# A listed order for all tasks, rounds of 768 and 1024 tokens, and sign bits by halfwords

## The chip, the cores and the metric

The kernel runs on one core of a Trainium2 chip. The metric is the device time of one execution in microseconds (us), the median of several runs. Five engines work side by side, each in the order in which its instructions were written: TensorE (PE in the profile, with weight loads as PEld) for matrix products into PSUM, VectorE (DVE) and ScalarE (ACT) for elementwise work, GpSimd (POOL) and SyncE (SP), which here only issue DMAs. Engines wait for each other through semaphores.

## The reference

```python
def _attn_ref(q, k, v, cap):                      # q, k, v: (4, 12, 448, 64)
    scores = (1 / sqrt(64)) * q @ k.T
    scores = cap * np.tanh(scores / cap)
    scores = scores - max(scores)
    attn = exp(scores); attn = attn / (sum(attn) + 1e-09)
    return attn @ v

def _moe_ref(x, w1, w2, w3, w_out):               # x: (1792, 768)
    a = x @ w1                                    # (1792, 1024)
    b = x @ w2
    h = a * b @ w3                                # w3: (1024, 1024)
    return h @ w_out                              # (1792, 768)
```

The heads of the attention's result are laid side by side to give x (4 batches of 448 tokens, 768 columns). Since nothing nonlinear stands between w3 and w_out, the kernel multiplies these two first.

## The kernel before, in words

**Work.** The 48 heads are taken as 24 pairs. For a pair, TensorE makes scores in tasks `S` (each float32 number is split into a high and a low part in the fp32r format, three products of the four are kept), ScalarE takes tanh (`H`) and exp (`E`), TensorE multiplies with v (`V`, `VJ`) and sums the exponentials (`T`, `Y`), a reciprocal goes through DRAM (`R0` to `R3`), VectorE scales (`N0`), and `N` stores the pair's 128 x 448 block to `x_dr`. Beside this, `O`, `Z` and `W` pieces bring w_out, w3, w1 and w2 from float64 words: a piece is loaded (`load`), its two 32-bit words are turned into one float (`low`, `sign`, `top`, `join`), and split into high and low (`high`, `out`). Tasks `C` multiply w3 with w_out and `D`, `DS` store the result.

**Rounds.** The products with w1 and w2 use Strassen's scheme with seven products, over two halves of the 768 channels and two blocks of tokens. A round covers two blocks: round 0 the batches 0 and 1, round 1 the batches 2 and 3, so a block has 448 tokens and a matmul 448 columns. `plan_xprep` loads a round's x from `x_dr`, forms the sums and splits them; `plan_moe` runs, for each of 8 column blocks m, seven products of three tasks `P` with three matmuls each, and combines them (`eM1`, `eo11`, ...), and `U` stores a*b to `u_dr`. Round 0 runs beside the end of the attention, round 1 after it; the split weights are stored to `w_dr` (`WS`) in round 0 and loaded again (`w1g`) in round 1.

**Last product.** `plan_out` takes 7 tiles of 256 tokens: loads from `u_dr` (`q`), sums (`s`), splits (`ha`, `la`), seven products of 4 tasks `p`, sums and stores to the output (`w`). Tile 4 takes its tokens from the ends of all four batches.

**Order.** Nothing of this is in loops at run time. Each step is a task with an engine (some with a second engine to choose), a duration, a key and needs. `Plan.run` plays the tasks through a model of the engines and writes each one's instructions when its engine takes it, the smallest key first; `SHIFTS` moves keys of single tasks. So the order of each engine's instructions is set when the program is built. TensorE works with four tile shapes: 128 x 128 (`C`, `P`, `p`), 64 rows x 128 (`S` on 128 keys), 64 x 64 (`S` on the last 64 keys, `VJ`) and 128 x 32 (`V`, `T`, `Y`). Stores named in `SHARED` can go by the SP queue or the GpSimd queue.

Of the kernel before, what the change touches and what calls it, by code (L numbers as in the profile page):

```python
# [37 lines left out]
class Slots:  # L38
# [9 lines left out]
    def close(self):  # L48
        self.uses[self.closed :] = sorted(
            self.uses[self.closed :], key=lambda x: (x[0] + x[2].shift, x[1])  # L50
        )
        for i in range(max(self.closed, self.n), len(self.uses)):
            new = self.uses[i][2]
            new.needs.extend(x for x in self.uses[i - self.n][3] if x is not new)
        self.closed = len(self.uses)


class Plan:
# [34 lines left out]
    def run(self, goals):  # L93
# [3 lines left out]
        for i, t in enumerate(self.tasks):  # L97
            t.key = (t.key + t.shift, i)
# [47 lines left out]
def program(  # L146
# [38 lines left out]
    SH = S // 2  # L185
    NRAW, NRT, NXS, NEV, NF = 3, 6, 5, 5, 6
# [3 lines left out]
    SIGN = -0x80000000  # L190
# [3 lines left out]
    const = ctx.enter_context(tc.tile_pool(name="const", bufs=1))  # L194
# [7 lines left out]
    ncap_sb = const.tile([P, 1], F32, name="ncap_sb")  # L202
    acap_sb = const.tile([P, 1], F32, name="acap_sb")
    wide_sb = const.tile([P, 1], F32, name="wide_sb")
    tsc_sb = const.tile([P, 1], F32, name="tsc_sb")
    ones = const.tile([P, P], F32, name="ones")
    ones2 = const.tile([P, P], F32, name="ones2")

# [23 lines left out]
    def put(name, eng, ns, key, emit, needs=(), lat=0.0, alt=(), after=()):  # L232
# [6 lines left out]
        done[name].shift = shifts.get(name, 0.0)  # L239
# [4 lines left out]
    class Piece:  # L244
# [7 lines left out]
        def load(self, pool):  # L252
# [3 lines left out]
            self.lo16 = self.raw.bitcast(U16)[:, : self.n, 1]  # L256
# [45 lines left out]
    def plan_piece(nm, x, key, lead, first=(), whole=True):  # L302

        n = x.n / PC
        for st, eng, ns, fn, needs, lat, alt in (
# [5 lines left out]
            ("sign", "DVE", 75 + 400 * n, x.sign, ("low",), 0, ()),  # L311
# [64 lines left out]
    att = ExitStack()  # L376
    qkp = att.enter_context(tc.tile_pool(name="qkp", bufs=2))
# [231 lines left out]

    def plan_X(pr):  # L610
# [19 lines left out]
        def total():  # L630
# [4 lines left out]
            for x, part in enumerate(parts):  # L635
                for n in range(4):
# [3 lines left out]
                        lhsT=ones[:, :32],  # L640
# [7 lines left out]
        def tail():  # L648
            for n in range(4):
# [3 lines left out]
                    lhsT=ones2[:, quarter(pr, j).start :][:, :32],  # L653
# [92 lines left out]
        def store():  # L746
            queue[0].dma_start(x_dr[pr], r[1])
# [4 lines left out]
        t = put(f"N{pr}", "SP", 450, end + 5, store, [f"N0{pr}"], 4500)  # L752
        use["x", pr].append(t)

    def plan_general(pr):

        def emit():
# [60 lines left out]
            queue[0].dma_start(x_dr[pr], xf)  # L818
# [14 lines left out]
    RT0, RWIN = (145, 328.18), (167.44, 104.0)  # L833
# [124 lines left out]
    def plan_xprep(r):  # L958

        tiles = {}  # L960
# [8 lines left out]
        def load(nm, kt, src, key, needs):  # L969
            x = nm, kt  # L970

            def emit():
                tiles[x] = xsp.tile([P, 512], F32, tag="xs", name=f"xs{r}{nm}{kt}")[:, :S]
                queue[0].dma_start(tiles[x], src)
# [5 lines left out]
        def keep_sum(kt):  # L980
            tiles["t1", kt] = ext[0].tile([P, S], F32, tag=f"t{kt}", name=f"t{kt}")

        def split(name, nm, kt, key, needs):
            i = op(name)

            def dst(x):
# [3 lines left out]
                return xt[r, i][:, kt, x, :S]  # L990

            def new(t):
# [3 lines left out]
                f"X{r}_{i}_{kt}", lambda: tiles[nm, kt], dst, S, key,  # L996
# [4 lines left out]
        def total(name, kt, to, a, b, key, needs):  # L1001
            def into():
# [6 lines left out]
                ALU.subtract, S, key, needs, [use["xs", r, x, kt] for x in {to, a, b}],  # L1009
# [3 lines left out]
        for kt in range(HX):  # L1013
# [14 lines left out]
            def keep(kt=kt):  # L1028
                queue[0].dma_start(t_dr[r, kt], tiles["a0", kt])
# [3 lines left out]
        for kt in range(HX):  # L1033
# [8 lines left out]
            total("T2", kt, "t1", "b1", "t1", key, [f"X{r}b1{kt}", f"X{r}T1{kt}" if r and kt else f"X{r}t1{kt}"])  # L1042
# [7 lines left out]
    def plan_moe(r, m):  # L1050
        box, ev, nm = {}, {}, f"{r}_{m}"
# [12 lines left out]
        def copy(name, bank, key, needs):  # L1064
            def emit(cp):
                ev[name] = evp.tile([P, S], F32, tag="ev", name=f"{name}{nm}")
                cp(ev[name], box[bank][:, :S])  # L1067

            evac(
                name, "ACT", 430, key, lambda: emit(nc.scalar.copy), needs, [bank], [name], True,  # L1070
                [("DVE", 540, lambda: emit(nc.vector.tensor_copy))],
            )

        def both(name, key, to, a, b, op, needs, banks=()):
            def emit():
                x = box[a][:, :S] if a in box else ev[a]
                y = box[b][:, :S] if b in box else ev[b]
                nc.vector.tensor_tensor(ev[to], x, y, op=op)

            evac(name, "DVE", 535, key, emit, needs, banks, sorted({x for x in (to, a, b) if x not in "ab"}))  # L1080

        def store(name, b, key, needs):
            def emit():
                queue[0].dma_start(u_dr[m, :, b * S : (b + 1) * S], ev[name])
# [4 lines left out]
        for i, p in enumerate(XORD):  # L1089
            bank = "a" if p in (1, 6, 7, 4) else "b"  # L1090
            new = p in (1, 2, 5)
            for kt in range(HX):

                def emit(p=p, i=i, kt=kt, bank=bank, new=new):
                    if new and kt == 0:
                        box[bank] = ps_o.tile([P, 512], F32, tag=tag[bank], name=f"pab{nm}_{p}")
                    for z, (a, c) in enumerate(((0, 0), (1, 0), (0, 1))):
                        nc.tensor.matmul(  # L1098
                            box[bank][:, :S],
                            lhsT=w_op(r, m, i)[:, a, kt, :],  # L1100
                            rhs=xt[r, i][:, kt, c, :S],
# [13 lines left out]
                t = put(f"P{nm}_{i}_{kt}", "PE", 612, key, emit, need)  # L1115
# [105 lines left out]
    def plan_C(n):  # L1221

        for nh in range(2):
# [30 lines left out]
            def evac(cp, box=box, c=c, nh=nh):  # L1254
                c[0] = evp.tile([P, S], F32, tag="ev", name=f"c{n}_{nh}")[:, :NH]
# [70 lines left out]
    def plan_out(t):  # L1326
# [4 lines left out]
        if t == 4:  # L1331
            at = [[(h * S + 3 * P, S - 3 * P), ((2 + h) * S + 3 * P, S - 3 * P)] for h in range(2)]
        else:
            r, i = (0, t) if t < 3 else (1, (0, 0, 0, 0, 0, 1, 2)[t])
            at = [[((2 * r + h) * S + i * P, P)] for h in range(2)]

        def load_quadrant(a, b):
            nm = f"A{a + 1}{b + 1}"

            def load():  # L1340
                ru[nm] = xsp.tile([P, HF, P], F32, tag="xs", name=f"{nm}_{t}")
                x = 0
                for t0, n in at[a]:
                    queue[0].dma_start(
                        ru[nm][:, :, x : x + n],
                        u_dr[b * HF : (b + 1) * HF, :, t0 : t0 + n].rearrange("m p t -> p m t"),
                    )
                    x += n
# [420 lines left out]
```

## Time and profile before

| what | value |
|---|---|
| median of 3 runs | 565.93 us (565.09 to 569.05) |
| the profiled execution's own time | 567.21 us |
| its span in the profile | 565.4 us |
| granted TensorE clock, mean | 0.996 |
| instructions | 10168 |
| DMA | 131.08 MB, mean 232 GB/s |

The span runs from the first to the last instruction of the profiled execution; some 1.8 us of its time lie outside. Busy time counts an instruction from its start to its end, and matmuls overlap each other; the chain of waits instead follows the work that ended last, and its pieces run from one start to the next.

### The profile page before, as it was taken

Reading aid. Unit: us, or ns where it says so; the run is one execution under the profiler, and the core shown is the slowest. Engines: PE = TensorE matmul, PEld = TensorE weight load, DVE = VectorE, ACT = ScalarE, POOL = GpSimd, SP = SyncE. Lnnn points to the kernel's source line nnn. Section 1 sums busy time; section 2 is a strip of 40 time slices with the busy share of each in tenths; the row PEclk is TensorE's granted clock in tenths of the full one; section 3 lists DMA queues with packets and bytes.
Section 4 is the critical chain, followed back from the end, with each engine's and each line's share of the span. In section 5 each row is a group of like instructions: output and inputs, shape, how many; then the busy total and the mean of one; then the engine's idle time right before and its main releaser. Section 6 shows DMA issues by size and latency. Waiting matters only on the chain.

```text
span 565.4 us, 10168 instructions
## 1 busy us (share of the span) xinstructions
PE 548.5 (97%) x3660; PEld 426.7 (75%) x3660; DVE 433.0 (77%) x874; ACT 342.6 (61%) x545; POOL 82.1 (15%) x150
## 2 busy tenths in 40 slices
PE   6999999999999999999999899999999999999994
PEld 3354558977576556667578889899999999999994
DVE  5998999687989999998987898765522676875531
ACT  6998998487978999887854654422211353344120
POOL 0000011101131111212213120111011001111311
PEclk9999999999999999999999999999999999999998
DMA  8678777758897876977579877899886233553311
GB/s 277 172 254 277 240 233 252 244 182 261 283 329 261 272 255 236 353 254 290 197 271 348 321 253 245 274 340 300 295 291 261 89 108 102 179 148 107 85 70 64
DMA packets 62510, 131.08 MB, mean 232 GB/s; under 512 B 12738, under 2 KB 40770, under 8 KB 60914
## 3 DMA queue, kind: packets, MB, share of 16 engines
q1 hardware_dynamic: 51746, 78.65, 44.2%
q0 software_dynamic: 10704, 51.68, 24.3%
q8 instruction: 31, 0.51, 0.4%
q14 instruction: 29, 0.24, 0.1%
HBM read 88.46 MB, written 41.77 MB: 230 GB/s over the span
## 4 chain that ended last, share of the span: by engine, by line
PE 73%; issue 9%; DVE 7%; DMA 5%; ACT 3%; POOL 1%; SPq 0%; POOLq 0%; DVEq 0%; ACTq 0%
PE pab L1098 35%; PE m L1452 13%; PE pv L555 7%; PE s L501 6%; PE pc L1233 6%; DMA r<-r_dr 3%; PE sum L638 2%; DMA r_dr<-z 1%; PE s L488 1%; PE pv L571 1%; PE sum L651 1%; ACT p L514 1%; POOL out_dram L1497 1%; DVE wt L344 1%; ACT p L517 1%
## 5 line engine op out<-in xcount | busy, mean ns | idle before, releaser
L517 ACT ACTIVATE p<-p,ncap_sb,acap_sb 128x896 f32<-128x896 f32 x84 | 92.6, 1138 | 0.1
L514 ACT ACTIVATE p<-s,tsc_sb 128x896 f32<-128x896 f32 x84 | 82.3, 1008 | 8.8 <-PE s L501 5.9
L1233 PEld LDWEIGHTS pc<-wo,w3t 128*128 128x128 f32 x384 | 65.6, 188 | 12.1 <-issue 5.9
L1233 PE MATMUL pc<-wo,w3t 128*128 128x384 f32 x384 | 73.3, 342 | 0.4 <-DVE wo L300 0.4
L1098 PE MATMUL pab<-x0T,wt 128*128 128x448 f32 x288 | 64.8, 371 | 2.4 <-ACT M L1067 2.3
L501 PE MATMUL s<-hl 64*128 64x448 f32 x432 | 58.9, 396 | 5.7 <-ACT hl L447 4.4
L1098 PE MATMUL pab<-x1T,wt 128*128 128x448 f32 x288 | 63.5, 368 | 0.1
L501 PEld LDWEIGHTS s<-hl 64*128 64x128 f32 x432 | 38.0, 190 | 33.6 <-ACT p L514 9.9
L555 PE MATMUL pv<-p,v 128*32 128x448 f32 x576 | 62.6, 546 | 0.6 <-ACT p L517 0.4
L1098 PEld LDWEIGHTS pab<-x0T,wt 128*128 128x128 f32 x288 | 52.8, 188 | 13.5 <-ACT M L1067 3.4
L1452 PE MATMUL m<-bT,ot 128*128 128x384 f32 x336 | 61.9, 334 | 0.0
L1452 PEld LDWEIGHTS m<-bT,ot 128*128 128x128 f32 x336 | 58.6, 188 | 0.1
L1098 PEld LDWEIGHTS pab<-x1T,wt 128*128 128x128 f32 x288 | 53.9, 188 | 5.8 <-ACT U L1067 0.4
L1098 PE MATMUL pab<-x0B,wt 128*128 128x448 f32 x216 | 48.7, 370 | 0.0
L1098 PE MATMUL pab<-x1B,wt 128*128 128x448 f32 x216 | 48.2, 368 | 0.0
L1452 PE MATMUL m<-bB,ot 128*128 128x384 f32 x252 | 47.1, 334 | 0.0
L1098 PEld LDWEIGHTS pab<-x0B,wt 128*128 128x128 f32 x216 | 39.7, 188 | 7.2 <-issue 1.7
L1384 ACT CAST ot<-A 128x512 fp32r<-128x512 f32 x40 | 23.6, 621 | 35.1 <-DVE A L1363 27.7
L1452 PEld LDWEIGHTS m<-bB,ot 128*128 128x128 f32 x252 | 44.0, 188 | 0.0
L1098 PEld LDWEIGHTS pab<-x1B,wt 128*128 128x128 f32 x216 | 40.5, 188 | 4.1
L1067 ACT COPY M<-pab 128x448 f32<-128x448 f32 x27 | 14.3, 531 | 39.4 <-PE pab L1098 39.2
L555 PEld LDWEIGHTS pv<-p,v 128*32 128x32 f32 x576 | 15.5, 109 | 28.8 <-issue 18.6
(143 smaller groups left out, 801.7 us busy)
## 6 DMA issues: line engine op xcount, KB each, us to landing
raw_w<-in_moe_w_dram SPq DMA_DIRECT2D x48, 384.0 KB
w_dr<-wt POOLq DMA_DIRECT2D x42, 384.0 KB, 4.5
wt<-w_dr POOLq DMA_DIRECT2D x10, 1536.0 KB, 7.7
kq<-in_kq_dram SPq DMA_DIRECT2D x23, 450.0 KB
raw_wo<-in_moe_w_out_dram SPq DMA_DIRECT2D x16, 384.0 KB
A<-u_dr SPq DMA_DIRECT2D x24, 256.0 KB
v<-in_v_dram SPq DMA_DIRECT2D x24, 224.0 KB
r<-r_dr SPq DMA_DIRECT2D x48, 112.0 KB
```

The source lines that it names most:

```text
L344: nc.vector.tensor_tensor(dst(1), src(), dst(0), op=ALU.subtract)
L488: nc.tensor.matmul(box[0][quarter(pr + n, j), n, :S], lhsT=raw_t[pr + n][at, QO + S + KM :], rhs=raw_t[pr + n][at, QO : QO + S], start=Tru ...
L501: nc.tensor.matmul(box[0][:, j, :S], lhsT=hl[at, a, S + (i - 1) * P : S + i * P], rhs=hl[at, c, :S], start=(z == 0), stop=(z == 2),)
L514: nc.scalar.activation(p, box[0][:, :, :S], AF.Tanh, scale=tsc_sb)
L517: nc.scalar.activation(p_t[pr, i], p_t[pr, i], AF.Exp, scale=acap_sb, bias=ncap_sb)
L555: nc.tensor.matmul(pv_t[pr][n * 32 : (n + 1) * 32, :S], lhsT=v_t[pr][:, 3 * j + i - 1, g * 32 : (g + 1) * 32], rhs=p_t[pr, i][:, j, :], st ...
L638: nc.tensor.matmul(box[1][n * 32 : (n + 1) * 32, :SH], lhsT=ones[:, :32], rhs=part[:, j, g * SH : (g + 1) * SH], start=(x == 0), stop=(x = ...
L1067: cp(ev[name], box[bank][:, :S])
L1098: nc.tensor.matmul(box[bank][:, :S], lhsT=w_op(r, m, i)[:, a, kt, :], rhs=xt[r, i][:, kt, c, :S], start=(new and kt == 0 and z == 0), stop ...
L1233: nc.tensor.matmul(box[0][:, :NH], lhsT=w3t[n][:, a, jt, :], rhs=wo[jt][:, c, ns], start=(jt == 0 and z == 0), stop=(jt == KF - 1 and z == 2),
L1384: copy(ot[j][:, q % 3, 0], ru[src])
L1452: nc.tensor.matmul(box[banks[m]][:, :NH], lhsT=ot[q // 3][:, q % 3, a, k, :], rhs=bt[RHS[m]][:, k, c, :], start=(new and k == 0 and z == 0 ...
```

## The change

The planner no longer chooses: all tasks are listed by name in the order in which they are written, with the engine after a slash where it is not the first one. There is one list up to the end of the attention and a second one for what follows. The rounds get blocks of 384 and of 512 tokens: round 0 takes the first 384 tokens of the batches 0 and 1, round 1 the whole batches 2 and 3 and, at the end of each block, the last 64 tokens of batch 0 or 1. The sign bits of a piece are masked from the upper halfword of the high word into the upper halfword of the low word, by an instruction with one tensor operand. The core of the diff:

```diff
+    SW = (384, 512)
+    OVER = S - SW[0]
+    UO = (0, SW[0], 2 * SW[0], 2 * SW[0] + SW[1])
...
-    shifts = {} if general else {
-        x.split(":")[0]: float(x.split(":")[1]) for x in SHIFTS.split()
-    }
+    part = iter(SEQUENCE.split("|"))
+
+    def run(goals):
+
+        if general:
+            plan.run(goals)
+            return
+        for x in next(part).split():
+            name, _, eng = x.partition("/")
+            opts = done[name].opts
+            opts[eng or next(iter(opts))][1]()
...
-            self.lo16 = self.raw.bitcast(U16)[:, : self.n, 1]
+            half = self.raw.bitcast(U16)[:, : self.n]
+            self.lo16, self.hi16 = half[:, :, 1], half[:, :, 3]
...
         def sign(self):
-            nc.vector.scalar_tensor_tensor(
-                self.lo, self.hi, SIGN, self.lo, op0=ALU.bitwise_and, op1=ALU.bitwise_or
-            )
+            nc.vector.tensor_scalar(self.lo16, self.hi16, 0x8000, None, op0=ALU.bitwise_and)
...
+    def keep_values(pr, x):
+
+        if pr >= PH:
+            queue[0].dma_start(x_dr[pr, :, :S], x)
+            return
+        queue[0].dma_start(x_dr[pr, :, : SW[0]], x[:, : SW[0]])
+        queue[0].dma_start(x_dr[pr + PH, :, S:], x[:, SW[0] :])
...
         def store():
-            queue[0].dma_start(x_dr[pr], r[1])
+            keep_values(pr, r[1])
...
                         nc.tensor.matmul(
-                            box[bank][:, :S],
+                            box[bank][:, :W],
                             lhsT=w_op(r, m, i)[:, a, kt, :],
-                            rhs=xt[r, i][:, kt, c, :S],
+                            rhs=xt[r, i][:, kt, c, :W],
...
-        if t == 4:
-            at = [[(h * S + 3 * P, S - 3 * P), ((2 + h) * S + 3 * P, S - 3 * P)] for h in range(2)]
-        else:
-            r, i = (0, t) if t < 3 else (1, (0, 0, 0, 0, 0, 1, 2)[t])
-            at = [[((2 * r + h) * S + i * P, P)] for h in range(2)]
+        r, i = (0, t) if t < 3 else (1, t - 3)
+        at = [[((2 * r + h) * S + i * P, P)] for h in range(2)]
+        if t == 6:
+            at = [[((x + h) * S + SW[0], OVER) for x in (2, 0)] for h in range(2)]
...
+SEQUENCE = """
+ld0 O0_1load O0_0load ld1 ldv0 O1_0load ldv1 ld2 h0_0/DVE l0_0 h0_1 cap S0_1 l0_1 O0_1low H0_1 S0_2
+O0_1sign O0_1top H0_2 S0_3 O0_1join O0_0top O1_1load E0_1 O0_0low S0_0 O0_0sign O0_0join H0_3
...
+P0_0_1_1 W2A21top eM1_0_0 W1S4 P0_0_1_2 E16_1 X0_2_1l P0_0_2_0 eo11_0_0 X0t12 P0_0_2_1 H16_0
+W2A21low N12 P0_0_3_0 l18_0 P0_0_3_1 O15 R114 E16_0 P0_0_3_2 W2A21sign R214 R115 S17_1 ld19 E16_3
+W2A21join S17_2 R215 X0_5_2h/DVE X0_4_1l WS0_5 eM5_0_0 V16_1 X0_5_2l W3A11load H17_1 W1_2l V16_2
...
+e422 p5_7_1 ha48/DVE w4M5 s6A12A12A11 p5_1_3 w3o12 p5_6_1 e5M1 p5_4_0 ha45 p4_4_3 ha46 p5_6_2 e421
...
+"""
```

Smaller edits that come with it: `x_dr` and `t_dr` get rows of 512 tokens, the evacuations and the x preparation use the round's width `W`, each quadrant of the last product is one load, the tiles `ones` and `ones2` shrink and live in the attention's pool. The second program in the file, for a large `cap`, is not entered with these inputs.

## Rows read from the trace of the kernel before

**Rows 1.** The page's first part: busy time, share of the span, instructions.
```profile
PE 548.5 (97%) x3660; PEld 426.7 (75%) x3660; DVE 433.0 (77%) x874; ACT 342.6 (61%) x545; POOL 82.1 (15%) x150
```

**Rows 2.** Windows by stage: length, each engine's busy time, granted clock, DMA share, GB/s.
```profile
0.00:40.00 40.00, 34.76 (x305) 17.10 (x305) 31.57 (x80) 35.16 (x45) 0.87 (x5) 1.00 0.73 233
40.00:95.00 55.00, 54.56 (x491) 30.42 (x491) 51.20 (x118) 52.04 (x73) 4.10 (x8) 1.00 0.80 251
95.00:195.00 100.00, 98.93 (x777) 70.61 (x776) 87.17 (x182) 78.94 (x123) 17.37 (x32) 1.00 0.78 260
195.00:351.00 156.00, 153.60 (x1000) 112.18 (x999) 143.00 (x284) 112.96 (x184) 29.83 (x51) 1.00 0.78 279
351.00:451.00 100.00, 99.94 (x484) 90.44 (x483) 53.09 (x100) 27.94 (x56) 12.05 (x22) 1.00 0.75 263
```

**Rows 3.** Chain of waits, 205 to 262 us: start, duration in us, what, matmuls.
```profile
206.15 1.41 PE s L501 x12
207.55 0.81 PE pab L1098 x3
...
212.06 0.52 PE sum L638 x8
...
213.44 0.38 PE sum L651 x8
...
218.16 0.91 PE s L488 x8
219.07 0.80 PE s L501 x6
...
230.82 2.39 PE pv L555 x24
...
239.36 6.27 PE pab L1098 x30
```

**Rows 4.** Chain of waits over the whole span, three of its pieces.
```profile
17.50 1.27 PE sum L638 x24
...
47.54 0.72 PE pc L1233 x3
...
461.53 69.18 PE m L1452 x399
```

**Rows 5.** Chain of waits, 395 to 440 us, in round 1.
```profile
394.85 45.25 PE pab L1098 x219
```

**Rows 6.** Timeline of TensorE, 0 to 12 us: start, us, line, tile, idle before.
```profile
4.40 0.74 PE L501 MATMUL s<-hl 64*128 64x448 f32 x2 [4.40 <-ACT hl L447]
...
7.60 1.77 PE L488 MATMUL s<-kq 64*64 64x448 f32 x8
```

**Rows 7.** Timeline of TensorE, 290 to 295 us.
```profile
292.58 0.56 PE L651 MATMUL sum<-p,ones 128*32 128x224 f32 x8
293.07 0.86 PE L1098 MATMUL pab<-x0T,wt 128*128 128x448 f32 x3
```

**Rows 8.** Timeline of TensorE, 550 to 566 us, its last row.
```profile
556.01 1.73 PE L1452 MATMUL m<-bB,ot 128*128 128x384 f32 x9
```

**Rows 9.** Groups by line and shape: count, busy us, mean ns, idle before.
```profile
L286 DVE SCALAR_TENSOR_TENSOR raw_w<-raw_w 128x384 int32<-128x384 int32 x48 | 26.1, 550 | 0.7 <-ACT raw_w L280 0.6
...
L275 DVE TENSOR_SCALAR raw_w<-raw_w 128x384 int32<-128x384 int32 x16 | 5.6, 352 | 0.2
...
L447 ACT CAST hl<-kq 128x576 fp32r<-128x576 f32 x1 | 0.7, 671 | 1.7 <-DMA kq<-in_kq_dram 1.7
```

**Rows 10.** Line 905, the weight stores: durations in ns as least, median, most.
```profile
L905 POOL DMA_DIRECT2D w_dr<-wt x42: 539/539/1199, 146.4 to 330.8; - x42
L905 SPq DMA_DIRECT2D w_dr<-wt x7: 320/331/380, 231.0 to 308.9; - x7
L905 SPq EVENT_SEMAPHORE  x6: 17/17/17, 230.4 to 306.3; - x6
```

**Rows 11.** Waits, longest first: us in total, times, longest us.
```profile
POOL w_dr L905 <- DVE wt L344: 64.3, 29, 9.5
...
POOL x_dr L747 <- DVE xf L744: 63.8, 15, 9.0
```

More of the change, by code (lines that the diff above doesn't have):

```diff
@@ L97, in run @@
         for i, t in enumerate(self.tasks):
[L98 removed]
+            t.key = (t.key, i)
             t.left = 0
@@ L376, in program @@
     att = ExitStack()
+    const = att.enter_context(tc.tile_pool(name="const", bufs=1))
+    ncap_sb = const.tile([P, 1], F32, name="ncap_sb")
+    acap_sb = const.tile([P, 1], F32, name="acap_sb")
+    wide_sb = const.tile([P, 1], F32, name="wide_sb")
+    tsc_sb = const.tile([P, 1], F32, name="tsc_sb")
+    ones = const.tile([P, 32], F32, name="ones")
+    ones2 = const.tile([P, 2, 32], F32, name="ones2")
     qkp = att.enter_context(tc.tile_pool(name="qkp", bufs=2))
@@ L751, in plan_X @@
         use["x", pr].append(t)
-        t = put(f"N{pr}", "SP", 450, end + 5, store, [f"N0{pr}"], 4500)
+        t = put(f"N{pr}", "SP", 450 if pr >= PH else 900, end + 5, store, [f"N0{pr}"], 4500)
         use["x", pr].append(t)
@@ L958, in plan_xprep @@
     def plan_xprep(r):
-        tiles = {}
+        tiles, W = {}, SW[r]
         def op(name):
@@ L972, in emit @@
             def emit():
-                tiles[x] = xsp.tile([P, 512], F32, tag="xs", name=f"xs{r}{nm}{kt}")[:, :S]
-                queue[0].dma_start(tiles[x], src)
+                tiles[x] = xsp.tile([P, 512], F32, tag="xs", name=f"xs{r}{nm}{kt}")[:, :W]
+                queue[0].dma_start(tiles[x], src[:, :W])
             t = put(f"X{r}{nm}{kt}", "SP", 450, key, emit, needs, 4000)
@@ L980, in keep_sum @@
         def keep_sum(kt):
-            tiles["t1", kt] = ext[0].tile([P, S], F32, tag=f"t{kt}", name=f"t{kt}")
+            tiles["t1", kt] = ext[0].tile([P, W], F32, tag=f"t{kt}", name=f"t{kt}")
         def split(name, nm, kt, key, needs):
@@ L1008, in total @@
                 f"X{r}{name}{kt}", into, lambda: tiles[a, kt], lambda: tiles[b, kt],
-                ALU.subtract, S, key, needs, [use["xs", r, x, kt] for x in {to, a, b}],
+                ALU.subtract, W, key, needs, [use["xs", r, x, kt] for x in {to, a, b}],
             )
@@ L1028, in keep @@
             def keep(kt=kt):
-                queue[0].dma_start(t_dr[r, kt], tiles["a0", kt])
+                queue[0].dma_start(t_dr[r, kt, :, :W], tiles["a0", kt])
             t = put(f"XT{r}{kt}", "SP", 450, key, keep, [f"X{r}T1{kt}"], 3500)
@@ L1041, in plan_xprep @@
             split("B21", "a1", kt, key, [f"X{r}a1{kt}"])
-            total("T2", kt, "t1", "b1", "t1", key, [f"X{r}b1{kt}", f"X{r}T1{kt}" if r and kt else f"X{r}t1{kt}"])
+            total("T2", kt, "t1", "b1", "t1", key, [f"X{r}b1{kt}", f"X{r}_{op('T1')}_{kt}l" if r and kt else f"X{r}t1{kt}"])
             split("T2", "t1", kt, key, [f"X{r}T2{kt}"])
@@ L1075, in emit @@
             def emit():
-                x = box[a][:, :S] if a in box else ev[a]
-                y = box[b][:, :S] if b in box else ev[b]
+                x = box[a][:, :W] if a in box else ev[a]
+                y = box[b][:, :W] if b in box else ev[b]
                 nc.vector.tensor_tensor(ev[to], x, y, op=op)
-            evac(name, "DVE", 535, key, emit, needs, banks, sorted({x for x in (to, a, b) if x not in "ab"}))
+            evac(name, "DVE", 70 + 1.04 * W, key, emit, needs, banks, sorted({x for x in (to, a, b) if x not in "ab"}))
         def store(name, b, key, needs):
             def emit():
-                queue[0].dma_start(u_dr[m, :, b * S : (b + 1) * S], ev[name])
+                queue[0].dma_start(u_dr[m, :, UO[b] : UO[b] + W], ev[name])
             t = put(f"U{b}_{m}", "SP", 700, key - 2, emit, [f"e{x}_{nm}" for x in needs], 4500)
@@ L1573, in program @@
             )
-        plan.run(goals)
+        run(goals)
         att.close()
```

358 lines of the change are left out of this document (223 added, 135 removed).

## The prediction, made before the changed kernel was run

> **What bounds the kernel now.** I read the busy line first: TensorE is busy 97% of the span, VectorE 77%, ScalarE 61% [rows 1]. A busy share is an average over stages, so the stages come next [rows 2]: in the reader's table TensorE has 2.4 us without work in the stage that holds round 0 (195 to 351 us), almost none in round 1 (351 to 451 us), and the granted clock is 1.00 (the 2.4 GHz level) in every stage shown. VectorE is busy 143 of 156 us in the round-0 stage and has room afterwards. So TensorE is the bound, with VectorE close behind it until round 1 starts.
>
> "Busy" there counts matmuls that overlap in the pipeline, so I price TensorE by the chain of waits instead, whose pieces run from start to start. In [rows 3] a task of round 0 (three matmuls of 448 columns) adds (6.27 - 0.81) / 9 = 0.607 us, and a piece of one task alone takes 0.81 us: 0.20 us are paid once for each stay, that is, each time TensorE comes to matmuls of this tile shape and leaves them again. In the same way: scores (64 rows by 128) 0.61 a task and 0.19 a stay; values and column sums (128 by 32) 0.75 and 0.38 a task and 0.14 a stay; the 64 by 64 tasks 0.91 with their stay; the products of w3 and w_out 0.72 alone [rows 4], which is 0.52 a task, by the price of long runs that follows, and 0.20 a stay. Long runs without a change of shape give 69.18 / 399 = 173.4 ns a matmul of 384 columns [rows 4] and 45.25 / 219 = 206.6 ns of 448 in round 1 [rows 5].
>
> Sum of TensorE's work: 72 scores x 0.61 = 43.9; 72 values x 0.75 = 54.0; 24 small tiles x 0.91 = 21.8; sums 42 x 0.38 + 6 x (1.27 - 0.14) = 22.7; w3 with w_out 128 x 0.52 = 66.6; round 0 168 x 0.607 = 102.0; round 1 168 x 0.62 = 104.1; last product 196 x 0.52 = 102.0; stays 40 x 0.20 + 44 x 0.19 + 48 x 0.14 = 23.1 (the shape changes 156 times, the first change is in [rows 6] and the last in [rows 7]; 24 of the stays are the small tiles', priced with them). That is 540.2 us. The first matmul starts at 4.40 [rows 6] and the last ends near 557.7 [rows 8], so about 13 us are waits, and 7.7 us follow the last matmul.
>
> **The change part by part.** My sum is made against the profiled execution, 567.21 us, which is 1.28 above the median 565.93; I take the difference off the median.
>
> *The listed order.* The tasks are the same 2,706; the list gives their order and engine. I counted the shapes in the list: 116 changes instead of 156. Stays of 128 by 128 matmuls 22 instead of 40, of scores 38 instead of 44, of values and sums 34 instead of 48, of small tiles 22 instead of 24. Saved: 18 x 0.20 + 6 x 0.19 + 14 x 0.14 = 6.7, and two small-tile stays, for which no row stands apart, between 0 and 0.2 each; I take 0.1, the middle of the other shapes' range. Together 6.9 us, all on the path, since TensorE has nearly no idle time to absorb it.
>
> *Rounds of 768 and 1024.* Each round keeps 504 matmuls; columns in total stay equal (384 + 512 = 2 x 448). Round 0 falls from 0.607 / 3 = 202.3 ns to the 173.4 that 384 columns take in two other loops with the same tile shape: 504 x 28.9 = 14.6 us off. Round 1 rises to a price that no row shows. Lower end: one column per cycle of the 2.4 GHz level and nothing else, 213.3 ns. Between: the 384 price and 128 more columns, 173.4 + 53.3 = 226.7 ns. Upper end: the line through 384 and 448 columns, 206.6 + 33.2 = 239.8 ns. I take 226.7: every run of 384 columns pays the same fixed 13.4 ns over its columns, while 448 pays between 15.6 (202.3 ns) and 19.9 (206.6 ns), so I read the surplus as belonging to 448 and not as growing with the columns. Round 1 then costs 504 x 20.1 = 10.1 us more (3.4 and 16.7 at the ends). Net 4.5 us off (11.2 off, 2.1 on).
>
> A 384-column matmul shows a fixed part of 13.4 ns [rows 4]. The Trainium skill (TensorE: Matmul & The Clock Gate, section "Back-to-back issue gap") gives the columns over 2.4 plus 2.5 ns, 162.5 ns for 384 and 216 for 512; the 384 row is 10.9 ns above that, so the measurement decides here. By the page's 216 ns, as an estimate, round 1 would cost 4.7 us more and the whole would end near 549 us.
>
> *The sign bits.* 64 operations of two operands on 384 columns and 8 on 256 become one-operand operations on halfwords. The one-operand shift on the same strided words takes 352 ns, the sign operation 550 [rows 9]. Saved at that price: 64 x 0.198, and 8 x 0.132 at two thirds of the columns, 13.7 us of VectorE; at the other end nothing, since no row has VectorE write halfwords. I take the first: the strides are those of the 352 ns row. VectorE is not the bound, so its direct worth is zero; it pays for what follows.
>
> *What VectorE is given.* Ahead of round 1's first matmul the list moves 31 one-operand pieces from ScalarE to VectorE (about 9 us), pushes 14 two-operand ones behind that matmul (8 us off) and narrows some 70 of round 0 by 64 columns (5 us off). With the sign bits: 143.0 + 87.2 + 51.2 + 31.6 = 313 us busy in 351 now [rows 2], or 0.892; then 313 - 13.7 - 4 = 295 us in 351 - 6.9 - 14.6 = 329.5, or 0.895. The cover is as thick as it was. ScalarE loses work nearly everywhere. In round 1 VectorE is busy 53 of 100 us now [rows 2], so the 512-column operations fit, and so, I take it, do 23 more conversions in the last product.
>
> *Queues.* Stores move from GpSimd's queue to SP's: in the first list SP issues 275 instead of 220 DMAs, GpSimd 24 instead of 79; in the second 122 instead of 83 and 24 instead of 63. An issue takes 0.33 us on SP and 0.54 on GpSimd [rows 10]. SP takes them in order: a store waits there for its data, and the loads listed behind it (raw weights, kq, the x tiles) wait with it; VectorE waits for those. Now GpSimd waits 2.2 us on average before a weight store and 4.3 before an x store [rows 11], with nothing behind it that anyone needs soon. I take 0 on the path.
>
> *Small edits, together 0.* The x tails add 12 small DMAs (12 x 0.33 us of issue, hidden). The last store becomes two (0.35 us at the end); the first conversion goes to VectorE, where 576 columns should take under its 671 ns on ScalarE, so TensorE may start up to 0.4 us earlier [rows 9]. I leave the 13 us of waits as they are, give or take 4: the ScalarE-bound start keeps its chain.
>
> Sum: -6.9 - 14.6 + 10.1 = -11.4 us, hence 565.9 - 11.4 = **554.5 us**.
>
> **Rivals.** (a) *512 columns cost 239.8 ns.* Net -6.9 + 2.1 = -4.8: 561.1 us. For it: the two widths on record lie on that line. Against: the constant surplus of 384.
>
> (b) *No fixed cost at 512.* If the fixed part hides behind a full-width matmul, it takes 213.3 ns: -6.9 - 14.6 + 3.4 = -18.1, 547.8 us. Every matmul of 384 columns speaks against it. The Trainium skill's formula above lies close to this case.
>
> (c) *Slower: the halfword operation costs what the word operation did.* Then VectorE has 309 us ahead of round 1, and at today's share of 0.892 needs 346.4 us instead of 329.5: 16.9 us of new waits before round 1, 571.4 us. It beats the whole gain once VectorE needs more than 329.5 + 11.4 = 340.9, at 304 us of work, that is, once a sign operation takes over about 480 ns. Against: the 352 ns rows.
>
> (d) *Slower: SP's queue holds the loads.* The list puts 32 more weight stores and 17 more x stores on SP; by the GpSimd waits that holds SP for up to 32 x 2.2 + 17 x 4.3 = 144 us. If over 8% of it reached TensorE the gain would be gone; at 12%, 17 us, it is 571.8 us. Against: seven weight stores already go by SP, and the waits on SP that stand before six of them took 17 ns each [rows 10]: listed late enough, a store holds nothing.
>
> GpSimd's weight stores take 0.54 us in the median and up to 1.20 [rows 10]. The Trainium skill (SBUF — State Buffer, "Who interferes with whom") says that one-operand VectorE operations take a port pair which GpSimd needs to write descriptors, and hold it for the whole instruction. By that rule the new sign operations would delay GpSimd's stores; only 48 DMAs are left there, so even 0.66 us on each, 32 us in all, lies on a queue that idles.
>
> **How the numbers follow.** Chances: forecast 0.65 (550 to 558.5 with the waits), (a) 0.12, (b) 0.08, (c) 0.06, (d) 0.09. The range takes in (a) and (b) with 2 us for the waits on either side: 547 to 563; (c), most of (d) stay out. One per cent (5.7 us), about what a measurement of this kernel can tell from no change, puts the borders at 560.3 and 571.6. (c) and (d) straddle the upper border, and I count most of them as slower: faster 0.75, same 0.13, slower 0.12.
>
> **What would show it.** In the profile after: 384-column matmuls of round 0 at 173 ns and 512-column ones at 227 ns from start to start in the chain; about 116 changes of shape; round 1's first matmul near 329 us; the halfword operation at about 350 ns; waits of TensorE not above 17 us; SP holding for stores without loads landing late. The prediction is wrong if round 1 runs at 240 ns, if VectorE's idle time vanishes before round 1, or if TensorE's waits grow by the amount of work saved.

## The result, and the profile after

The changed kernel takes 552.21 us (median of 4 runs, 551.79 to 553.52) against 566.1 for the kernel before beside it (565.09 to 569.05): a ratio of 0.975, 95% interval 0.971 to 0.979. The forecast was 554.5 us in a range of 547 to 563.

The page's first part, which answers to [rows 1]:

```profile
span 550.0 us, 10061 instructions
...
PE 535.8 (97%) x3660; PEld 423.4 (77%) x3660; DVE 458.8 (83%) x948; ACT 306.2 (56%) x471; POOL 27.5 (5%) x54
```

TensorE is as full as before, of a span shorter by 15.4 us. VectorE is 26 us busier over the whole span. Ahead of round 1, where the forecast took 18 us off it (13.7 + 4), it has 308 us of work instead of 313: only 5 us less. The windows, with the columns of [rows 2]; the stages end earlier now:

```profile
0.00:40.00 40.00, 34.69 (x348) 18.70 (x352) 35.66 (x94) 34.76 (x40) 0.20 (x4) 1.00 0.76 247
40.00:95.00 55.00, 54.99 (x484) 35.14 (x477) 52.87 (x125) 45.09 (x64) 0.00 (x0) 1.00 0.83 252
95.00:195.00 100.00, 100.00 (x812) 72.42 (x813) 94.40 (x201) 86.64 (x128) 6.61 (x12) 1.00 0.80 260
195.00:327.00 132.00, 131.22 (x948) 102.77 (x948) 128.79 (x265) 100.63 (x166) 8.12 (x15) 1.00 0.90 302
```

Between 195 and 327 us VectorE is busy 128.79 of 132 us, 97.6%, and TensorE still works for 131.22 of them. Before, VectorE stood at 92% of its round-0 stage [rows 2]. The chain of waits, which answers to [rows 3 to 5]:

```profile
270.24 6.45 PE pab L1116 x36
...
279.84 39.42 PE pab L1116 x222
319.81 114.46 PE pab L1116 x507
443.01 98.93 PE m L1466 x570
```

The first piece is round 0, 384 columns, one stay: (6.45 - 0.20) / 36 = 173.6 ns a matmul. The third holds the last 27 matmuls of round 0 and 480 of round 1, which have 512 columns, so its mean (114.46 / 507 = 225.8 ns) mixes the two. Inside round 1, 446 of the 496 steps from one start to the next take 226 or 227 ns, 226.7 in the mean. The last piece is the last product with 98.93 / 570 = 173.6 ns, near the 173.4 of [rows 4]. Round 1's first matmul starts at 323.1 us (351.2 before).

The groups by line and shape, for [rows 9]; the sign operations are line 290, and line 277 is the shift from which they were priced:

```profile
L290 DVE TENSOR_SCALAR raw_w<-raw_w 128x384 uint16<-128x384 uint16 x48 | 28.9, 603 | 0.4
...
L277 DVE TENSOR_SCALAR raw_w<-raw_w 128x384 int32<-128x384 int32 x25 | 9.0, 360 | 0.0
...
L290 DVE TENSOR_SCALAR raw_wo<-raw_wo 128x384 uint16<-128x384 uint16 x16 | 9.7, 620 | 0.1
...
L290 DVE TENSOR_SCALAR raw_w<-raw_w 128x256 uint16<-128x256 uint16 x8 | 3.7, 458 | 0.3 <-ACT raw_w L282 0.3
```

The halfword operation takes 603 ns where 352 was forecast and the word operation took 550. The timeline's end:

```profile
540.84 1.17 SPq L1511 DMA_DIRECT2D out_dram<-U  x2
541.97 0.48 ACT L1444 COPY o<-m 128x384 f32<-128x384 f32 x1 [14.08 <-PE m L1466]
542.47 1.17 SPq L1511 DMA_DIRECT2D out_dram<-o  x2
```

**A ledger for every kernel.** A busy share can't say whether TensorE works or waits inside its pipeline, so I walked the starts of the 3,660 matmuls of each trace. Each task has the price that the prediction took from [rows 3 to 7], to the nanosecond (540.7 us in all for before, not 540.2), with 3 x 226.7 ns for a 512-column task; what a step takes beyond its price is a wait. So the work is price times count and not a measurement of its own (the pieces of the chain above and e5 test the prices), and a wait holds everything else, time at a lower granted clock too. First is the start of the first matmul, tail what follows the last one; first, work, waits and tail add up to the span, all in us of the profiled run:

| kernel | first | work | waits | of these, 195 to 327 us | tail | span | median |
|---|---|---|---|---|---|---|---|
| before | 4.4 | 540.7 | 12.4 | 3.5 | 7.8 | 565.4 | 566.1 |
| after | 4.3 | 529.1 | 8.4 | 3.1 | 8.2 | 550.0 | 552.2 |
| e1 word sign | 4.2 | 529.1 | 7.6 | 2.5 | 8.2 | 549.1 | 551.9 |
| e2 list, 896 twice | 4.4 | 533.8 | 6.3 | 0.0 | 6.6 | 551.2 | 553.0 |
| e3 old order, 768 | 4.4 | 536.1 | 23.1 | 12.9 | 8.9 | 572.4 | 574.2 |
| e4 old, halfword sign | 4.6 | 540.7 | 12.3 | 3.6 | 7.9 | 565.6 | 565.9 |
| e5 40 more changes | 4.2 | 536.8 | 8.0 | 2.5 | 8.4 | 557.4 | 558.5 |
| e6 stores on GpSimd | 4.1 | 529.1 | 15.0 | 8.3 | 8.0 | 556.2 | 557.9 |
| e7 engines of before | 4.4 | 529.1 | 18.8 | 6.2 | 7.9 | 560.3 | 561.5 |
| e8 whole last store | 4.1 | 529.1 | 8.6 | 2.5 | 6.8 | 548.6 | 550.7 |
| e9 no sign | 4.1 | 529.1 | 5.7 | 1.1 | 8.5 | 547.4 | 549.2 |
| e10 old, 768, no sign | 4.4 | 536.1 | 20.3 | 11.4 | 8.7 | 569.5 | 571.4 |
| e12 old, 768, SP stores | 4.3 | 536.1 | 22.6 | 11.3 | 8.7 | 571.6 | 577.7 |

The change as a whole is work -11.6, waits -4.1, tail +0.4, first matmul -0.1. By the same walk some 3 of the 4 us of waits vanish before 195 us.

### The profile page after: what moved, and what is told of

The parts are those of the page before. It is cut to its first block, busy times and chain, and to the rows that moved or that the text cites. A ratio compares the mean times of both kernels' runs of the same rounds, so it can differ in the third digit from the quotient of the medians.

```text
span 550.0 us, 10061 instructions
## 1 busy us (share of the span) xinstructions
PE 535.8 (97%) x3660; PEld 423.4 (77%) x3660; DVE 458.8 (83%) x948; ACT 306.2 (56%) x471; POOL 27.5 (5%) x54
## 4 chain that ended last, share of the span: by engine, by line
PE 85%; DVE 7%; DMA 3%; ACT 2%; issue 1%; SPq 0%; DVEq 0%
PE pab L1116 32%; PE m L1466 19%; PE pc L1251 13%; PE pv L565 8%; PE s L511 7%; PE sum L656 2%; PE pv L581 2%; PE sum L669 1%; PE s L498 1%; DMA kq<-in_kq_dram 1%; DVE wt L346 1%; DMA raw_w<-in_moe_w_dram 1%; DVE a L639 1%; ACT p L524 1%; DVE t_w L293 1%
## 5 line engine op out<-in xcount | busy, mean ns | idle before, releaser
L1116 PE MATMUL pab<-x1T,wt 128*128 128x512 f32 x288 | 71.2, 390 | 0.0
L1251 PE MATMUL pc<-wo,w3t 128*128 128x384 f32 x384 | 70.6, 339 | 0.0
L1466 PE MATMUL m<-bT,ot 128*128 128x384 f32 x336 | 66.7, 334 | 0.0
L1116 PEld LDWEIGHTS pab<-x1T,wt 128*128 128x128 f32 x288 | 53.9, 188 | 11.3 <-ACT M L1085 0.4
L1116 PE MATMUL pab<-x0T,wt 128*128 128x384 f32 x288 | 55.9, 338 | 0.0
L1116 PE MATMUL pab<-x1B,wt 128*128 128x512 f32 x216 | 54.4, 390 | 0.0
L1116 PEld LDWEIGHTS pab<-x0T,wt 128*128 128x128 f32 x288 | 49.9, 188 | 3.3 <-issue 1.7
L1466 PE MATMUL m<-bB,ot 128*128 128x384 f32 x252 | 51.6, 334 | 0.0
L1116 PE MATMUL pab<-x0B,wt 128*128 128x384 f32 x216 | 42.6, 340 | 0.0
L290 DVE TENSOR_SCALAR raw_w<-raw_w 128x384 uint16<-128x384 uint16 (+1 forms) x56 | 32.6, 582 | 0.6 <-ACT raw_w L282 0.3
L293 DVE SCALAR_TENSOR_TENSOR t_w<-t_w,raw_w 128x384 int32<-128x384 int32 (+1 forms) x56 | 29.8, 537 | 2.8 <-ACT t_w L272 1.5
```

The costliest lines, as they stand in the source:

```text
L290: nc.vector.tensor_scalar(self.lo16, self.hi16, 0x8000, None, op0=ALU.bitwise_and)
L293: nc.vector.scalar_tensor_tensor(self.t, self.t, 3, self.lo, op0=ALU.logical_shift_left, op1=ALU.bitwise_or)
L1116: nc.tensor.matmul(box[bank][:, :W], lhsT=w_op(r, m, i)[:, a, kt, :], rhs=xt[r, i][:, kt, c, :W], start=(new and kt == 0 and z == 0), stop ...
L1251: nc.tensor.matmul(box[0][:, :NH], lhsT=w3t[n][:, a, jt, :], rhs=wo[jt][:, c, ns], start=(jt == 0 and z == 0), stop=(jt == KF - 1 and z == 2),
L1466: nc.tensor.matmul(box[banks[m]][:, :NH], lhsT=ot[q // 3][:, q % 3, a, k, :], rhs=bt[RHS[m]][:, k, c, :], start=(new and k == 0 and z == 0 ...
```

## The experiments

Four kernels ran in each of three groups on the same chip as the kernel before; its median was 566.2 in the first, 567.4 in the second and 565.5 in the third, so a ratio is the safer number across groups.

**e1_word_sign: the changed kernel with the sign operation of before.**

```diff
-            nc.vector.tensor_scalar(self.lo16, self.hi16, 0x8000, None, op0=ALU.bitwise_and)
+            nc.vector.scalar_tensor_tensor(
+                self.lo, self.hi, SIGN, self.lo, op0=ALU.bitwise_and, op1=ALU.bitwise_or
+            )
```

> The changed kernel with the sign bits again by the word operation of two operands. The profile after shows the halfword operation at 603 to 620 ns against 550 for the word one. Theory A (TensorE sets the pace, VectorE's cover holds even at 129 of 132 busy us in the round-0 stage): no difference within 1 us, 552 us. Theory B (VectorE at 98% busy has begun to set the pace there): 72 operations get some 50 to 60 ns cheaper, up to 3.8 us, 548.5 us. Theory C (the halfword form pays in some way the group's mean does not show): slower, 554 or more.

Measured: 551.86 us, ratio 0.9745 (0.9704 to 0.9785). The sign edit gives nothing in the changed kernel.

**e2_list_896: the list and the halfword sign, both rounds with 896 tokens.**

```diff
-    SW = (384, 512)
+    SW = (448, 448)
```

(With it, one store of x to `x_dr` instead of two, and the output tiles of before.)

> The changed kernel with both rounds at 896 tokens again (list and halfword sign kept, the last product's tile 4 takes the ends of the batches as before). Theory A (matmul prices alone): round 0 gives back 504 x (202 to 207 less 173.4) = 14.6 to 16.7 us and round 1 loses 504 x 20.1 = 10.1, so 4.5 to 6.6 us more, 556.7 to 558.8 us. Theory B (the width does nothing, columns in total are equal): 552 us. Theory C (the list fits only the new rounds, so waits come with the old ones): 560 or more.

Measured: 552.95 us, ratio 0.9756 (0.9717 to 0.9794). Beside the list the widths are worth 0.7 us by the medians, 0.3 by the ratios and 1.2 by the spans, which the intervals do not tell from nothing. That is theory B's number, but not its reason: by the ledger, with the forecast's prices, they take 533.8 - 529.1 = 4.7 us off TensorE's work, but some 2 of it come back as waits and 1.6 in the tail. Two pieces of this kernel's chain, round 0 and round 1:

```profile
286.90 45.79 PE pab L1112 x225
...
399.37 38.36 PE pab L1112 x186
```

448 columns take 203.5 ns in round 0 and 206.2 in round 1, as in [rows 3] and [rows 5]: the higher price goes with the place and not with the list.

**e3_order_before_768: before's order written as a list, rounds of 768 and 1024 tokens, word sign.**

```diff
+    SW = (384, 512)
```

(with the edits for the widths that come with it, and the sequence that the planner of before had made, in place of the planner)

> The order of before, written as a list, with rounds of 768 and 1024 tokens and the word sign: the widths alone. Theory A: the matmul prices give 4.5 to 6.6 us, 559.5 to 561.6 us, and the shape still changes 156 times. Theory B (the gain of the width needs the new order, since round 0 gets shorter and VectorE is then late for round 1): 566 or more.

Measured: 574.17 us, ratio 1.0143 (1.0096 to 1.0190). Theory B by its number: the same widths that gain 1.2 us at most in the new order lose 8 in the old one. TensorE's work is 4.7 us less here too; the waits grow by 10.7 us, 9.4 of them between 195 and 327 us. ScalarE's timeline shows where:

```profile
300.22 0.48 ACT L1088 COPY M<-pab 128x384 f32<-128x384 f32 x1
...
301.84 0.99 ACT L273 ACTIVATE t_w<-raw_w 128x384 f32<-128x384 f32 x2
308.97 0.62 ACT L346 CAST x1B<-xs1a 128x512 fp32r<-128x512 f32 x1 [6.14 <-DMA x_dr<-xf]
...
311.94 0.47 ACT L1088 COPY M<-pab 128x384 f32<-128x384 f32 x1
```

ScalarE stands for 6.14 us at the first conversion of round 1's tokens, which have yet to come through DRAM; the copy of a finished product out of PSUM (`M<-pab`) is listed behind it. TensorE's own list of waits names that copy:

```profile
PE pab L1119 <- ACT M L1088: 4.2, 3, 2.9
PE pab L1119 <- DVE M L1099: 3.3, 2, 2.6
```

In the kernel before, the same two steps of ScalarE stand so:

```profile
306.43 0.53 ACT L1067 COPY M<-pab 128x448 f32<-128x448 f32 x1
...
312.12 0.57 ACT L341 CAST x1B<-xs1a 128x448 fp32r<-128x448 f32 x1 [3.02 <-issue]
```

The copy of round 0 comes 6.2 us earlier with the narrower matmuls, the converted tokens only 3.1: the place of the conversion fits a longer round 0. VectorE stands in the same way, 4.46 us, for a reciprocal that goes through DRAM, with a result of round 0 behind it:

```profile
302.29 0.63 DVE L765 TENSOR_TENSOR xf<-xf,r 128x448 f32<-128x448 f32 x1 [4.46 <-DMA r<-r_dr]
...
305.57 0.55 DVE L1099 TENSOR_TENSOR M<-M,pab 128x384 f32<-128x384 f32 x1
```

From 300 to 316 us the waits are some 5 us longer than before. TensorE stands for 2.55 us and, after one run of matmuls, for 2.88, and around the end of the second stand the granted clock falls to 0.50 (the 1.2 GHz level):

```profile
312.00:315.40 3.40, 2.93 (x9) 2.93 (x10) 3.40 (x7) 1.03 (x3) 0.04 (x1) 0.50 0.85 233
```

A matmul of 384 columns takes 320 ns there, so some 1.5 of the 5 us are clock and not queues. The other half of the 10.7 us is spread over the stages up to round 1.

**e4_halfword_before: the kernel before with the halfword sign alone.** The edit of e1, reversed.

> The kernel before with the halfword sign alone (the planner is left as it was). Theory A (VectorE has room in the old order: 0.89 busy ahead of round 1): 566 us within 1.5. Theory B (it is on the path): 72 operations some 50 ns longer, 3.7 us, 569.8 us.

Measured: 565.87 us, ratio 0.9989 (0.9960 to 1.0018). No difference. GpSimd's weight stores (first line: before; second: e4, one line number less) got longer all the same:

```profile
L905 POOL DMA_DIRECT2D w_dr<-wt x42 | 24.0, 571 | 80.2 <-DVE wt L344 64.3 <-issue 7.6 <-ACT U L1067 3.4
```

```profile
L904 POOL DMA_DIRECT2D w_dr<-wt x42 | 26.1, 622 | 80.0 <-DVE wt L343 64.2 <-issue 7.6 <-ACT U L1066 3.4
```

The sign operation is the only instruction that differs, and an issue takes 51 ns more in the mean, 2 us in all on a queue that idles. Most do not change (the median is 542 ns against 539); the mean comes from the nine of 42 that take over 600 ns, three before. The direction is that of the rule of the Trainium skill (SBUF — State Buffer, "Who interferes with whom") that the prediction weighed: one-operand VectorE operations can, in their two-port modes, hold ports that GpSimd needs for its descriptors. The prediction had left that condition out. In the changed kernel, with ten weight stores left on GpSimd, an issue takes 543 ns.

**e5_more_changes: the changed kernel with 156 changes of shape instead of 116.** One of the 20 moves, in the list:

```diff
-O6_0top S5_1 H5_2 O4_1sign O6_0sign C0_0_3 O6_0join O3 C0_1_3
+O6_0top C0_0_3 S5_1 H5_2 O4_1sign O6_0sign O6_0join O3 C0_1_3
```

> The changed kernel with 20 of its 128x128 tasks moved past one neighbour on TensorE, so that the shape changes 156 times, as often as in the kernel before, instead of 116; everything else, the widths, engines and queues included, is the changed kernel's. Theory A, a stay costs what the rows of before gave (0.20 us for 128x128, 0.19 scores, 0.14 values and sums, 0.1 small tiles): 20 x 0.20 + 16 x 0.19 + 3 x 0.14 + 0.1 = 7.6 us more TensorE work and waits as they are, 559.8 us against the changed kernel's 552.2. Theory B, the changes are mostly hidden beside waits and the gain of the list came from elsewhere: under 2 us, 554 or less.

Measured: 558.51 us, ratio 0.9842 (0.9815 to 0.9868). That is 6.3 us by the medians, 0.9% or 5.2 us by the ratios, 7.4 by the spans: most of the 7.6 expected. In this kernel's chain a round-0 task alone takes 0.73 us where three matmuls in a run take 0.52:

```profile
201.66 0.73 PE pab L1116 x3
```

**e6_stores_gpsimd: the changed kernel's list with the queues of before.** For 108 DMAs, as here:

```diff
-V3_2 N0 O4_0sign N01
+V3_2 N0/POOL O4_0sign N01
```

> The changed kernel's list with each of 108 DMAs back on the queue (SP or GpSimd) that it had before, 101 of them stores that return to GpSimd. Theory A, the queues carry nothing of the gain: 551.2 to 553.2 us, the waits of TensorE stay near 8.4 us. Theory B, the 4.1 us of waits that vanished did so because stores left GpSimd's queue: they come back, about 556 us.

Measured: 557.93 us, ratio 0.9828 (0.9793 to 0.9864). Theory B, which the prediction did not have: the move to SP's queue is worth some 5 us. GpSimd's timeline, and then the chain of waits from there:

```profile
294.43 0.54 POOL L623 DMA_DIRECT2D x_dr<-xf  x1 [8.78 <-DVE xf L762]
295.03 0.54 POOL L1102 DMA_DIRECT2D u_dr<-M  x1
```

```profile
294.43 0.54 POOL x_dr L623
295.03 6.87 DMA u_dr<-M
301.97 0.49 ACT M L1085
302.50 5.52 PE pab L1116 x21
```

The x store holds GpSimd's queue for 8.78 us because its data come late, but the store behind it, `u_dr<-M`, loses only some 0.5 us by that: VectorE ends its result at 294.5 us, and the store is issued at 295.03. What is long is its landing, 6.87 us. The tile comes free at 301.9 us, only then does ScalarE copy the next product out of PSUM, and only then does TensorE go on, after 1.80 us without work. In the changed kernel SP issues the same store and nobody waits for its landing: the copy, 5.5 us after the issue, waits for TensorE.

```profile
293.94 0.55 DVE L1096 TENSOR_TENSOR M<-M,pab 128x384 f32<-128x384 f32 x1
```

```profile
292.31 0.68 SPq L1102 DMA_DIRECT2D u_dr<-M  x1
...
297.77 0.48 ACT L1085 COPY M<-pab 128x384 f32<-128x384 f32 x1 [0.56 <-PE pab L1116]
```

(The first line is of e6, the other two of the changed kernel.) A second `u_dr<-M` on GpSimd's queue, issued at 332.14 us, lands after 7.92 us, and TensorE waits again, 0.8 us. After the first stand the granted clock is 0.50 (the 1.2 GHz level) from 303.9 to 307.3 us:

```profile
303.90:307.30 3.40, 3.40 (x13) 3.40 (x12) 2.49 (x5) 1.90 (x4) 0.00 (x0) 0.50 0.64 208
```

A matmul of 384 columns takes 320 ns there, which is some 1.5 us of waits. The stretch from 283 to 308 us and the second place together hold some 6 of the 6.6 us by which the waits grow. Why stores on GpSimd's queue land that late is not shown.

**e7_compute_engines: the changed kernel's list with the 186 choices between VectorE and ScalarE of before.** As here:

```diff
-Z0_1top O1_1high/DVE Y1 O2_1low
+Z0_1top/ACT O1_1high Y1 O2_1low
```

> The changed kernel's list with each of the 186 pieces that changed between VectorE and ScalarE back on the engine that it had before. Theory A, the position in the list frees VectorE's time, not the choice of engine: VectorE's work ahead of round 1 falls by some 9 us, TensorE's waits stay within 2 us of 8.4, 551 to 554 us. Theory B, the choice of engine took the waits away: they return to the 12.4 us of before or more, 556 us or above, with the new waits on pieces that ScalarE finishes late.

Measured: 561.53 us, ratio 0.9894 (0.9865 to 0.9924). Theory B. VectorE has 303.4 us of work ahead of round 1 instead of 308.0 and 333.8 us to do it in; the waits grow by 10.4 us, spread over all stages up to round 1. TensorE's list of waits puts 5.0 us of them, besides the first, down to ScalarE (1.5 in the changed kernel) and 3.9 to VectorE (0.2), so theory B's reason holds for half. Its longest lines:

```profile
PE s L511 <- ACT hl L457: 4.4, 1, 4.4
PE sum L656 <- DVE a L641: 1.9, 2, 1.5
PE s L511 <- ACT p L524: 1.7, 3, 0.7
PE pv L565 <- ACT p L527: 1.5, 3, 1.0
```

(The first is the wait before the first matmul, which every kernel has.)

**e8_tail: word sign, and the output tile whose stores are two DMAs each no longer last.**

```diff
-        r, i = (0, t) if t < 3 else (1, t - 3)
+        r, i = (0, t) if t < 3 else (1, (0, 3, 1, 2)[t - 3])
...
-        if t == 6:
+        if t == 4:
```

> The changed kernel with the two-operand sign operation on words, and with the output tile that straddles two stretches of tokens (its stores are two DMAs each) made the fifth instead of the last, so that the last store is one DMA. Theory A, the split store is what lengthens the tail (8.2 us after the last matmul against 6.6 where both rounds had 896 tokens): 1.6 us less, 550.3 us. Theory B, the tail is the drain of stores whatever their number: no change, 551.9 us.

Measured: 550.73 us, ratio 0.9708 (0.9681 to 0.9736), the fastest complete kernel here. The tail falls from 8.2 us (in the changed kernel and in e1, which has the same sign operation) to 6.8; its last line now is one issue:

```profile
542.54 0.33 SPq L1514 DMA_DIRECT2D out_dram<-o  x1
```

The interval overlaps that of the changed kernel, so the 1.4 us rest on the two timelines, not on the medians.

**e9_no_sign_after: the changed kernel without sign operations.**

> The changed kernel without its sign operations (the sign bits of the weights are left out of the words, so the products use other weights); 72 operations, some 43 us, less on VectorE. Theory A, the 3.1 us that TensorE still waits between 195 and 327 us are VectorE's lack of time: they fall below 1 us and the time to 549 to 550 us. Theory B, they come from loads and from pieces in the way on ScalarE: above 551.5 us.

Measured: 549.18 us, ratio 0.9711 (0.9679 to 0.9742). Theory A, nearly to its number: the waits between 195 and 327 us fall from 3.1 to 1.1 us. VectorE's window there:

```profile
195.00:320.30 125.30, 125.23 (x925) 99.50 (x922) 114.98 (x234) 96.65 (x159) 8.13 (x15) 1.00 0.90 306
```

43 us of VectorE work are worth 2.2 us of time by the ratios and 3.0 by the medians: that is all that a VectorE at 97.6% cost.

**e10_no_sign_old_order: e3 without sign operations.**

> The order of before with rounds of 768 and 1024 tokens (574.2 us) without its sign operations (the sign bits are left out, so the products use other weights); 72 operations, some 39 us, less on VectorE. Theory A, the 9 us of new waits in round 0 of that order are VectorE running at its limit of 0.89 of the time: they vanish, about 565 us. Theory B, they are the fixed places in the queues of ScalarE and VectorE: a conversion of round 1's tokens stands ahead of evacuations that TensorE needs, and waits for its tokens to come through DRAM, whatever VectorE has to do: above 571 us.

Measured: 571.43 us, ratio 1.0102 (1.0069 to 1.0135). Theory B: 39 us less work on VectorE give back 2.8 us, and ScalarE's gap at the same conversion is still 5.39 us. (The granted clock is 0.50 from 304.9 to 311.7 us here, twice as long as in e3, which hides a little more than 1 us of what was given back.)

**e11_sign_forms: the sign operation in five forms.** In turn, with `q` and `q2` dense stretches of halfwords:

```diff
+            if k == 0:
+                nc.vector.tensor_scalar(lo16, hi16, 0x8000, None, op0=ALU.bitwise_and)
+            elif k == 1:
+                nc.vector.tensor_scalar(q, hi16, 0x8000, None, op0=ALU.bitwise_and)
+            elif k == 2:
+                nc.vector.tensor_scalar(lo16, q, 0x8000, None, op0=ALU.bitwise_and)
+            elif k == 3:
+                nc.vector.tensor_scalar(q2, q, 0x8000, None, op0=ALU.bitwise_and)
```

(and for k = 4 words with a step of two)

> The changed kernel with its sign operations cut to 288 of 384 columns and taken in turn in five forms (so the words are not the weights): halfwords with a step of four to the same, with a step of four to dense ones, dense to a step of four, dense to dense, and one operand of 32-bit words with a step of two. At three quarters of the measured durations the first takes 0.75 x 603 = 452 ns and the last, by the shift's 352 ns, 264. Theory A, the step of four costs where halfwords are written: the two forms that write with a step take about 450 ns and the two dense writes under 300. Theory B, it costs where they are read: the two that read with a step take 450. Theory C, it costs halfwords as such: all four take about 450.

Measured, 553.45 us in one run; the groups by line and shape (lines 299, 301, 303, 305, 307 for k = 0 to 4):

```profile
L303 DVE TENSOR_SCALAR raw_w<-raw_w 128x288 uint16<-128x288 uint16 x10 | 4.9, 490 | 0.0
L299 DVE TENSOR_SCALAR raw_w<-raw_w 128x288 uint16<-128x288 uint16 x8 | 3.9, 487 | 0.0
L301 DVE TENSOR_SCALAR raw_w<-raw_w 128x288 uint16<-128x288 uint16 x11 | 3.4, 308 | 0.6 <-ACT raw_w L284 0.2 <-ACT t_w L274 0.2
...
L307 DVE TENSOR_SCALAR raw_w<-raw_w 128x288 int32<-128x288 int32 x9 | 2.7, 297 | 0.0
L305 DVE TENSOR_SCALAR raw_w<-raw_w 128x288 uint16<-128x288 uint16 x10 | 2.2, 217 | 1.1 <-ACT t_w L274 1.1
```

Theory A. Halfwords written with a step of four take 487 to 490 ns however they are read; written densely they take 308 and 217; words with a step of two 297. It is the halfword write with a step that costs; the read with a step costs 91 ns where the write is dense. Whether it is the step, or that only half of each 32-bit word is written, was not tried apart.

**e12_old_order_sp_stores: e3 with the queues of the changed kernel.** The edit of e6 in the other direction, in before's order.

> The order of before with rounds of 768 and 1024 tokens (574.2 us) and the changed kernel's choice of queue for 108 DMAs, 101 of them stores that go from GpSimd's queue to SP's. Theory A, that order's waits stand behind the tokens' way through DRAM and not behind stores on GpSimd: 572 to 576 us. Theory B, they are the stores queued behind one another on GpSimd, as in the changed kernel with these stores put back (5.7 us slower): 568.5 us or less.

Measured: 577.65 us, ratio 1.0212 (1.0184 to 1.0241); the profiled run took 573.36. Not theory B: the queues of the new list give nothing in the old order, and at 3.5 us above e3 (and above theory A's 576) perhaps cost something, which the profiled run doesn't show. In it ScalarE's first conversion of round 1's tokens starts at 305.44 us, after a gap of 2.64 us where e3 had 6.14, and still the waits are 22.6 us against 23.1: the one place in e3's timeline is not the whole of the loss.

## Why the prediction was right, and where its parts were wrong

**The bound: right.** TensorE's work, forecast to fall by 11.4 us, falls by 11.6 of the 15.4 that the span loses. Both are sums of the same prices; what bears them out are the 173.6 and 226.7 ns of the chain and the 40 changes of e5.

**The list, -6.9 by 40 changes of shape: right as a term, half of what the list does.** e2 against before has 6.9 us less work, and e5, which puts 40 changes back and moves nothing else far, returns 6.3 us by the medians, 5.2 by the ratios. But the list alone (e2) gains 13.2 us: it also takes 6.1 us of waits and 1.2 of tail away. I had left the waits "as they are, give or take 4".

**The widths, net -4.5: each price right, the net not received.** 384 columns cost 173.6 ns and 512 columns 226.7, so rivals (a) with 239.8 and (b) with 213.3 fall; the constant 13.4 ns over the columns was the right reading. The Trainium skill's 216 ns for 512 columns (TensorE: Matmul & The Clock Gate, "Back-to-back issue gap"), which stands there for an isolated matmul, a condition that the prediction left out, is 10.7 ns below what round 1 shows, much as for 384. What failed is the step from TensorE's work to time: round 0 ended earlier, and what had to be ready by then did not. In the list that costs some 2 us of waits, about what goes when VectorE has 43 us less to do (e9), and the output tile that straddles two stretches costs 1.6 more. In the old order it costs 10.7 us and turns the gain into 8 us of loss; there about half lies where data on their way through DRAM stand at fixed places of the queues (e3), and not VectorE's amount of work (e10).

**The sign operation, 352 ns: wrong.** It takes 603, since the row that I took writes words, and the cost lies in writing halfwords with a step (e11). No row showed that write, and I had named the other end as "nothing saved"; a loss belonged in the range. On the time it is nothing in either kernel (e1, e4).

**VectorE at 0.895 ahead of round 1, rival (c): its condition came true, its consequence not.** VectorE had 308 us of work, beyond the 304 from which I said the gain would be gone, and did it in 323.1: 0.953. I had taken "today's share of 0.892" as what VectorE can reach. It is what the old order lets it reach: e3 has 308 of 346.8 us, 0.888, and taking 39 us of work off (e10) hardly helps. In the list VectorE comes closer to its limit, and 43 us of work cost 2 to 3 us of time (e9). "If VectorE's idle time vanishes before round 1" was one of the prediction's signs of being wrong: of the 132 us between 195 and 327 it had 3.2 idle, and the time held all the same.

**The queues, 0 on the path: wrong, and with the sign opposite to rival (d).** "With nothing behind it that anyone needs soon" is the sentence that failed: on GpSimd's queue there were result stores whose tiles the next copies out of PSUM needed, and with the stores put back there the time is 4.4 to 5.7 us longer (e6). The prediction had asked how long a store holds the queue; in the place that the trace shows, the hold costs 0.5 us and the landing is what TensorE waits for. Rival (d) falls with that: with the stores on SP's queue the kernel is faster, not slower.

**The engines.** I counted what VectorE is given and found the cover as thick; that the moves themselves gain was not in the sum. Undone, they cost 8.2 to 9.3 us (e7).

**Small edits.** TensorE starts 0.1 us earlier, not up to 0.4. The last store as two costs 1.4 to 1.6 us, not 0.35: I had counted the second issue (1.17 for two against 0.33) at the least duration of one, and not the later landing.

So the total was near because TensorE's work was summed rightly, and because two things outside the sum partly cancelled, which is luck: beside its work the list takes 7.3 us away (e2), and the widths give back 3.6 of them. Queues (e6) and engines (e7), each undone alone, cost more than the 4.1 us that the waits fell by, so their shares don't add; and the queues moved into the old order gain nothing (e12). What is shown is that order, engines and queues work together; how much of the waits each took away alone stays open. So does why e12 runs above e3.

## What to carry to other kernels

Price the work on the bound engine from long runs in the trace, and then ask of every piece that comes earlier which in-order queue holds what it needs: a faster stretch under an order made for the slower one can lose more than it gains. An engine's busy share under one order is no ceiling for another. For a store, ask not who reads the data but whose next buffer waits for it to land, and look at the one place, not at the mean.

## What the runs showed of the hardware that was not expected

- A VectorE operation on 288 halfwords takes 487 to 490 ns where it writes with a step of four, 308 where only the read has the step, 217 dense to dense; on words with a step of two 297 (e11).
- After stands of TensorE of 1.8 to 2.9 us the granted clock fell from 1.00 to 0.50 (from the 2.4 to the 1.2 GHz level) for 3.4 us (e3, e6), and a 384-column matmul took 320 ns instead of 174; in the changed kernel it never did.
- Two stores of 192 KB on GpSimd's queue landed 6.87 and 7.92 us after their issue (e6).
- With VectorE 97.6% busy for 132 us, TensorE was busy for 131.2 of them, with 3.1 us of waits by the ledger (after).
- The last store of an execution, as two DMAs instead of one, moved the end by 1.4 us from the last matmul (after against e8).
